# Attention feeding a balanced expert layer: a new order for the tiles, the q turns and the writes of the attention stage

## The chip, the cores and the metric

The kernel runs on one core of a Trainium2 chip. The metric is the device time of one execution in microseconds (us), and the median of several runs is compared. The profile is one more execution, taken by the hardware profiler; its times are in microseconds from the start of its span, except where ns is written. PE is TensorE (matmuls and transposes), DVE is VectorE, ACT is ScalarE, POOL is GpSimd, and SP is the engine whose queue issues most of the transfers.

## The reference

```python
# q, k, v: (8 batches, 8 heads, 576 rows, 64), float32
kv  = einsum('bhsd,bhse->bhde', k, v)            # a 64 x 64 matrix for each head, no softmax
out = einsum('bhsd,bhde->bhse', q, kv)
rms = sqrt(mean(out * out, axis=-1) + 1e-6)
x   = out / rms * g_norm                         # then (B, S, H*D) = 4608 tokens of 512
logits = x @ w_gate                              # 8 experts
# tokens go to experts greedily, best logit first, each expert takes exactly 576
for e in range(8):
    out[mask_e] = relu(x[mask_e] @ w1[e]) @ w2[e]  # 512 -> 1024 -> 512
```

## The kernel before

The kernel has three stages. The attention stage (the first 121 us of the profile) computes x, without the factor g_norm, and the logits. It writes x to the DRAM tensor `x_dram`. Then a search on VectorE finds the threshold of the first expert and its list of tokens. From about 160 us on, eight expert layers run on TensorE, each with rows gathered from `x_dram`; searches for the later experts run beside them. The change is in the attention stage.

There, `load` issues one transfer of 576 KB for half of the heads of q, k or v of one batch. Each of the six halves has two buffers. All loads and all writes of x go through SP's queue in program order, and `paced` lets each of them start only after the third one before it has landed. The loads of batches 0 and 1 are issued at the top. The later ones are issued by `again` inside `prepare`, two batches ahead, as soon as the buffer's last reader stands in the program.

`prepare(b)` is a generator that does all that batch b needs before its tiles:

- `sum_kv(r)`, for four pairs of heads, sums k-transposed times v into the PSUM tile `kv_ps` (L395). ScalarE copies the upper half of it as `odd` (L415), VectorE adds the lower half to make `kv` (L417), and GpSimd copies that into `kvx` (L423).
- `turn_q(n)`, for n from 0 to 4, transposes four blocks of q (two in the last) into the PSUM tile `qt_ps` (L380) and copies them into `qt`, on VectorE for n = 1 and 2 and on ScalarE else.
- `kv` is transposed into `t_ps` (L431), copied by ScalarE as `kvt` (L433), and multiplied by the gate's weights in `w_ps` (L442), which VectorE copies into the last 8 columns of `kvx` (L444). So one product of q with `kvx` gives the output and the parts of the logits.

`qt_ps`, `t_ps` and `w_ps` share the two PSUM buffers of the tag `tr`. The generator yields four times, and the main loop takes one piece of it after each tile.

`tiles(c0, rows)` gives the functions `one`, `scale` and `logits` for the tiles of a batch. A tile has 128 rows of a batch, all eight heads. A batch of 576 rows has four and a half, so every odd batch has a fifth tile, with the last 64 rows of the batch before it and its own. `one(t, ...)` makes 16 matmuls into `o_ps` (32 for the tile of two batches, L479); ScalarE squares them as `sq` (L485) and copies them into `o_sb` (L486); VectorE sums the squares into `ms` (L490). `scale` turns all sums of the batch into the factors `inv` (L494 to L498). `logits` adds up the logits `lg` (L503, L506), and multiplies `o_sb` by `inv` into `xo`: for batches 0 to 6 on GpSimd at once (L511), and for the last on ScalarE, put off until after the loop (`late`, L516). Writes of `xo` are collected in `writes` and issued when eight or more are waiting, the oldest first (L520).

`ones(n)` makes matmuls of constants whose result nobody reads (L361). `chore` runs one piece of a list of small VectorE work for the search: first its set-up, then, from batches 2, 4 and 6 on, `early` for nine columns of `lg` in four pieces; the last of these (L303, L335) compares them with 32 candidates into `over_c`. PE, DVE, ACT and SP take their instructions in the order of the program here; POOL's order is left to the scheduler.

The main loop is:

```python
for b in range(B):
    parts = prepare(b + 1) if b + 1 < B else iter(())
    ...
    for t in range(len(rows)):
        one(t, copies, {0: 1, 3: 2}.get(t, 0))
        next(parts, None)
        if b < 2 or t == 3 or b == 6 and t == 2:
            chore()
    ...
    scale()
    logits()
```

Of the kernel before, what the change touches and what calls it, by code (L numbers as in the profile page):

```python
# [7 lines left out]
FT = mybir.dt.float32  # L8
# [7 lines left out]
P = 128  # L16
# [10 lines left out]
def kernel(  # L27
# [14 lines left out]
    B, H, S, D = q.shape  # L42
# [4 lines left out]
    HP = P // 2  # L47
    R = S // HP
    GC = N // P
    DC = DM // P  # L50
    FC = F // P
    W = D + E
# [12 lines left out]
    att = att_cm.__enter__()  # L65
# [22 lines left out]
            loaded[name, b, h].rearrange("p r j d -> p r (j d)"),  # L88
            src[b].rearrange("h s d -> (h s) d").rearrange("(r p j) d -> p r (j d)", r=NP, j=R)[:, rs]))

    for b in range(2):
        for h in range(2):
            for name in "kvq":
                load(name, b, h)

    ones_b = asg.tile([P, P], BF, name="ones_b")
    nc.vector.memset(ones_b, 1.0)
# [252 lines left out]
    def chore(times=1):  # L350

        for _ in range(times):
            if chores:
                chores.pop(0)()
# [12 lines left out]
    def prepare(b):  # L367

        k_sb, v_sb, q_sb = ([loaded.pop((name, b, h)) for h in range(2)] for name in "kvq")
        q_sb = [x.rearrange("p r j d -> p (r j d)") for x in q_sb]  # L370
        NT = NP * R // 2
        qt = att.tile([P, 2, NT, HP], FT, name="qt", tag="qt", bufs=3)
        turned_q[b] = qt

        def turn_q(n):
            m = min(4, NT - 4 * n)
            t_ps = psa.tile([P, 4, P], FT, name="qt_ps", tag="tr", bufs=2)
            for x in range(m):
                h, at = divmod(4 * n + x, NT // 2)
                nc.tensor.transpose(t_ps[:, x, :], q_sb[h][:, at * P:(at + 1) * P], ident)  # L380

            to, got = qt[:, :, 4 * n:4 * n + m], t_ps[:, 0:m].rearrange("p x (l c) -> p l x c", l=2)
            if n in (1, 2):
                nc.vector.tensor_copy(to, got)
            else:
                nc.scalar.copy(to, got)


        kv_ps = psa.tile([P, 2, 512], FT, name="kv_ps", tag="kv")

        def sum_kv(r):
            for j in range(R):
                for l in range(2):
                    ls, cs = slice(l * D, (l + 1) * D), slice(j % 2 * D, (j % 2 + 1) * D)
                    nc.tensor.matmul(kv_ps[cs, l, r * D:(r + 1) * D], lhsT=k_sb[r // 2][ls, r % 2, j, :], rhs=v_sb[r // 2][ls, r % 2, j, :],  # L395
                                     start=(j < 2), stop=(j >= R - 2))

        def again(names, h):
            if b + 2 < B:
                for name in names:  # L400
                    load(name, b + 2, h)

        if b > 0:
            ones(2, kv_ps[:, 0, :])
        for r in range(2):
            sum_kv(r)
            if r:
                again("kv", 0)
            turn_q(r)
            yield  # L410
        sum_kv(2)
        sum_kv(3)
        again("kv", 1)
        odd = att.tile([D, 2, NP * D], FT, name="odd", tag="odd")
        nc.scalar.copy(odd, kv_ps[D:P, :, 0:NP * D])  # L415
        kv = att.tile([D, NP, 2, D], FT, name="kv", tag="kv")
        nc.vector.tensor_tensor(kv.rearrange("p r l d -> p l r d"),  # L417
                                kv_ps[0:D, :, 0:NP * D].rearrange("p l (r d) -> p l r d", d=D),
                                odd.rearrange("p l (r d) -> p l r d", d=D), op=AL.add)

        kvx = att.tile([P, H, W], FT, name="kvx", tag="kvx", bufs=3)
        for n in range(2):
            nc.gpsimd.tensor_copy(kvx[n * D:(n + 1) * D, :, 0:D], kv.rearrange("p r l d -> p (r l) d"))  # L423
        if b == 0:
            ones(5)
        yield
        turn_q(2)
        again("q", 0)
        t_ps = psa.tile([P, NP, D], FT, name="t_ps", tag="tr", bufs=2)
        for r in range(NP):  # L430
            nc.tensor.transpose(t_ps[:, r, :], kv[:, r].rearrange("p l d -> p (l d)"), ident[0:D, 0:D])  # L431
        kvt = att.tile([P, NP, D], FT, name="kvt", tag="kvt")
        nc.scalar.copy(kvt, t_ps)  # L433
        yield
        turn_q(3)
        if b == 0:
            nc.vector.tensor_scalar(gw.rearrange("p r l e -> p (r l e)"), in0=gw.rearrange("p r l e -> p (r l e)"),
                                    scalar1=g_col, scalar2=None, op0=AL.mult)
        w_ps = psa.tile([P, NP, 2 * E], FT, name="w_ps", tag="tr", bufs=2)
        for r in range(NP):  # L440
            for n in range(2):
                nc.tensor.matmul(w_ps[n * D:(n + 1) * D, r], lhsT=kvt[:, r, :],  # L442
                                 rhs=gw[:, r].rearrange("p l e -> p (l e)"), start=True, stop=True)
        nc.vector.tensor_copy(kvx[:, :, D:W], w_ps.rearrange("p r (l e) -> p (r l) e", l=2))  # L444
        kv_of[b] = kvx
        turn_q(4)
        again("q", 1)

    LAG = 4
    writes, late = [], []  # L450
    last_own = GC - (R + 1) // 2

    def tiles(c0, rows):


        T = len(rows)
        o_sb = att.tile([P, T, H, W], FT, name="o_sb", tag="o_sb", bufs=2)
        xo = att.tile([P, T, H, D], FT, name="xo", tag="xo", bufs=LAG + 1)
        ms = att.tile([P, T * H], FT, name="ms", tag="ms")
        rt = att.tile([P, T * H], FT, name="rt", tag="rt")  # L460
        inv = att.tile([P, T * H], FT, name="inv", tag="inv")
        own = c0 + T <= last_own

        def one(t, copies, fill):

            o_ps = psa.tile([P, 2, 512], FT, name="o_ps", tag="o", bufs=2)
            ones(fill, o_ps[:, 0, :])
            for r2 in range(NP // 2):
                for l in range(2):
                    for rp in range(2):  # L470
                        r = 2 * r2 + rp
                        at = [slice(h * HP, (h + 1) * HP) for h in range(2)]
                        halves = rows[t]
                        parts = [(slice(0, P), halves[0], 2)] if halves[0][0] == halves[1][0] else [
                            (at[n], half, 1) for n, half in enumerate(halves)]
                        for rows_at, (bn, j), m in parts:
                            block = R * r + j
                            ks = slice(block % 2 * D, (block % 2 + 1) * D)
                            nc.tensor.matmul(  # L479
                                o_ps[rows_at, rp, (2 * r2 + l) * W:(2 * r2 + l + 1) * W],  # L480
                                lhsT=turned_q[bn][ks, l, block // 2:block // 2 + m].rearrange("p x c -> p (x c)"),
                                rhs=kv_of[bn][ks, 2 * r + l], start=True, stop=True)
            o4 = o_ps[:, :, 0:NP * W].rearrange("p b (h w) -> p b h w", w=W)
            sq = att.tile([P, H, D], FT, name="sq", tag="sq")
            nc.scalar.activation(sq.rearrange("p (b h) d -> p b h d", b=2), o4[:, :, :, 0:D], ACT.Square, scale=D ** -0.5)  # L485
            copies.append(lambda: nc.scalar.copy(o_sb[:, t].rearrange("p (b h) w -> p b (h w)", b=2), o_ps[:, :, 0:NP * W]))  # L486
            if own or t != T - 2:
                while copies:
                    copies.pop(0)()
            nc.vector.reduce_sum(out=ms[:, t * H:(t + 1) * H], in_=sq, axis=AXX)  # L490
# [38 lines left out]
    with tc.manual_schedule(engines={PE, DVE, ACTE, SPE}):  # L529
        ones(18)  # L530
        for _ in prepare(0):
            pass
        for b in range(B):
            parts = prepare(b + 1) if b + 1 < B else iter(())
            rows = [((b, j), (b, j + 2)) for j in (0, 1, 4, 5)]
            if b % 2:
                rows.append(((b - 1, R - 1), (b, R - 1)))
            one, scale, logits = tiles(b // 2 * R + b % 2 * (R // 2), rows)
            copies = []
            if b in choose_at:  # L540
                early(*choose_at[b])
            for t in range(len(rows)):
                one(t, copies, {0: 1, 3: 2}.get(t, 0))
                next(parts, None)
                if b < 2 or t == 3 or b == 6 and t == 2:
                    chore()
            for _ in parts:
                pass
            if b + 1 == B:
                while chores:  # L550
                    chore()
            scale()
            logits()
            if b < B - 1:
                chore(2 if b == 6 else 1)

            while len(writes) >= 2 * LAG:
                writes.pop(0)()
        early(27, GC)
        while chores:  # L560
            chore()
        for do in late:
            do()
        while writes:
            writes.pop(0)()
# [683 lines left out]
```

## Time and profile before

| | |
|---|---|
| median of 3 runs | 658.64 us (658.54 to 659.15) |
| the profiled execution: its own time, its span | 660.36 us, 658.6 us |
| mean granted TensorE clock | 0.968 |
| busy: PE, DVE, ACT, POOL | 605.8, 387.8, 194.5, 389.3 us |
| read from HBM, written | 71.32 MB, 18.87 MB |
| loads of q, k, v: 48 transfers | 576 KB each, 5.8 to 6.1 us from issue to landing |
| writes of x: 20 transfers | 512 or 256 KB, 4.0 to 4.4 us |

A line of the timeline has the start, the duration, the engine, the line of the program, the operation, what is written and from what, the shape, the count, and in brackets how long the engine had been idle before it and what ended that. In the windows table each stretch has the busy time of each engine in it, then the clock that was granted to TensorE as a share of full speed, the share of time that the DMA engines were busy, and the rate. The search stage and the attention stage have different limits, so shares of the whole span say little about either.

### The profile page before, as it was taken

The page shows a single profiled execution, that of the slowest core. Times are in us where ns is not written, and L with a number is a line of the kernel's source. Part 1 is how long each engine was busy: PE and PEld are TensorE (multiplying, and loading weights), DVE is VectorE, ACT ScalarE, POOL GpSimd, SP SyncE. Part 2 cuts the span into 40 slices and gives each one's busy share as a digit, 9 for nine tenths or more (in the row PEclk, how much of TensorE's full clock was granted, in tenths as well). Part 3 has the DMA queues.
Part 4 walks back from the last instruction along what each step waited for, and adds up shares of the span by engine and source line. Part 5 has one row for each costly group of instructions (what it writes and reads, how often), then busy time and mean ns, then how long its engine had stood idle before and what let it go on. Part 6 is the DMA issues. An engine that isn't in the chain of part 4 may idle for free.

```text
span 658.6 us, 12759 instructions
## 1 busy us (share of the span) xinstructions
PE 605.8 (92%) x4932; PEld 464.6 (71%) x4932; DVE 387.8 (59%) x1249; ACT 194.5 (30%) x395; POOL 389.3 (59%) x405
## 2 busy tenths in 40 slices
PE   7989998335899999999999999999999999999994
PEld 4767777232678677867786786778678867877873
DVE  4466667778678588668757956976671053123201
ACT  1555665611131223123212222231223123222300
POOL 1035434104585487749846974887388669848822
PEclk9999999657999999999999999999999999999998
DMA  8999989416306402710442072109103620721001
GB/s 270 310 315 295 292 291 340 154 50 199 128 0 204 164 33 71 257 41 33 158 171 73 1 262 99 41 0 323 46 32 100 229 72 1 279 84 37 0 9 64
DMA packets 49852, 91.02 MB, mean 138 GB/s; under 512 B 3712, under 2 KB 20096, under 8 KB 49792
## 3 DMA queue, kind: packets, MB, share of 16 engines
q1 hardware_dynamic: 43200, 71.31, 31.6%
q0 software_dynamic: 5888, 18.88, 8.3%
q8 instruction: 39, 0.64, 0.4%
q14 instruction: 21, 0.17, 0.1%
q10 hardware_dynamic: 704, 0.02, 0.1%
HBM read 71.32 MB, written 18.87 MB: 137 GB/s over the span
## 4 chain that ended last, share of the span: by engine, by line
PE 77%; DVE 9%; DMA 5%; issue 4%; ACT 3%; POOL 1%; POOLq 0%; SPq 0%; DVEq 0%; ACTq 0%
PE x_ps L1065 13%; PE x_ps L1025 11%; PE z_ps L1065 9%; PE y_ps L1065 9%; PE z_ps L1025 7%; PE y_ps L1025 7%; PE o_ps L479 4%; PE y_ps L1127 4%; PE kv_ps L395 3%; PE t_ps L969 3%; PE qt_ps L380 2%; DMA v_sb<-in_v_dram 2%; DMA q_sb<-in_q_dram 2%; PE given_ps L651 1%; PE given_ps L646 1%
## 5 line engine op out<-in xcount | busy, mean ns | idle before, releaser
L1070 ACT COPY h<-x_ps 128x288 f32<-128x288 f32 x93 | 37.2, 400 | 166.5 <-PE x_ps L1065 153.7
L1065 PE MATMUL x_ps<-xs,sw 128*128 128x288 f32 x248 | 71.3, 409 | 0.0
L875 POOL DMA_INDIRECT xg<-x_dram,ids x40 | 38.1, 952 | 51.8 <-DMA w_sb<-in_moe_w_dram 37.7
L992 POOL DMA_INDIRECT out_dram<-y_sb,outs x32 | 31.5, 983 | 55.8 <-DVE y_sb L1163 41.1
L1025 PE MATMUL x_ps<-tw,sh 128*128 128x256 f32 x256 | 61.6, 384 | 0.0
L972 ACT ACTIVATE xt<-t_ps,g_col 128x512 f32<-128x512 f32 (+1 forms) x40 | 25.7, 645 | 110.9 <-PE t_ps L969 110.9
L1065 PEld LDWEIGHTS x_ps<-xs,sw 128*128 128x128 f32 x248 | 46.2, 190 | 14.3 <-issue 1.7
L955 POOL TENSOR_TENSOR sw<-w_sb 128x256 f32<-128x256 f32 x64 | 46.8, 731 | 12.3 <-PE z_ps L1065 9.6
L1017 POOL TENSOR_TENSOR sh<-hid 128x512 f32<-128x512 f32 x32 | 40.7, 1272 | 19.9 <-ACT hid L1040 19.9
L1025 PEld LDWEIGHTS x_ps<-tw,sh 128*128 128x128 f32 x256 | 46.9, 190 | 7.1 <-issue 0.8
L1040 ACT ACTIVATE hid<-hid 128x576 f32<-128x576 f32 x64 | 43.8, 686 | 22.9 <-DVE hid L1079 13.1
L511 POOL TENSOR_TENSOR xo<-o_sb,inv 128x512 f32<-128x512 f32 x31 | 32.9, 1090 | 29.7 <-DVE inv L498 16.6
L1103 POOL TENSOR_TENSOR tw<-w_sb 128x512 f32<-128x512 f32 x32 | 40.1, 1276 | 5.0 <-DMA w_sb<-in_moe_w_dram 5.0
L479 PEld LDWEIGHTS o_ps<-kvx,qt 64*128 64x128 f32 (+1 forms) x640 | 33.7, 181 | 12.0 <-issue 7.1
L479 PE MATMUL o_ps<-kvx,qt 64*128 64x72 f32 (+1 forms) x640 | 38.9, 274 | 3.4 <-ACT o_sb L486 3.4
L1065 PE MATMUL z_ps<-xt,sw 128*128 128x288 f32 x128 | 37.8, 413 | 0.1
L1065 PE MATMUL z_ps<-xs,sw 128*128 128x288 f32 x128 | 37.0, 409 | 0.0
L1065 PE MATMUL x_ps<-xt,w_sb 128*128 128x288 f32 x124 | 36.8, 414 | 0.1
L1065 PE MATMUL y_ps<-xt,w_sb 128*128 128x288 f32 x128 | 36.9, 409 | 0.0
L1065 PE MATMUL y_ps<-xs,w_sb 128*128 128x288 f32 x128 | 36.7, 408 | 0.0
L490 DVE TENSOR_REDUCE ms<-sq 128x8 f32<-128x512 f32 x36 | 24.3, 683 | 20.1 <-ACT sq L485 19.8
L423 POOL COPY kvx<-kv 64x512 f32<-64x512 f32 x16 | 9.7, 607 | 43.9 <-DVE kv L417 26.9
(278 smaller groups left out, 1332.4 us busy)
## 6 DMA issues: line engine op xcount, KB each, us to landing
w_sb<-in_moe_w_dram SPq DMA_DIRECT2D x32, 512.0 KB, 5.7
w_sb<-in_moe_w_dram SPq DMA_DIRECT2D x8, 2048.0 KB, 14.3
k_sb<-in_k_dram SPq DMA_DIRECT2D x16, 576.0 KB, 5.8
v_sb<-in_v_dram SPq DMA_DIRECT2D x16, 576.0 KB, 5.8
q_sb<-in_q_dram SPq DMA_DIRECT2D x16, 576.0 KB, 6.1
x_dram<-xo SPq DMA_DIRECT2D x16, 512.0 KB, 4.4
x_dram<-xo SPq DMA_DIRECT2D x4, 256.0 KB, 4.0
xg<-x_dram,ids POOLq DMA_INDIRECT x40, 5.4
```

What stands on the lines that cost most here:

```text
L479: nc.tensor.matmul(o_ps[rows_at, rp, (2 * r2 + l) * W:(2 * r2 + l + 1) * W], lhsT=turned_q[bn][ks, l, block // 2:block // 2 + m].rearrange ...
L511: nc.gpsimd.tensor_tensor(xo[:, t], o_sb[:, t, :, 0:D], inv[:, t * H:(t + 1) * H].rearrange("p (h o) -> p h o", o=1).to_broadcast([P, H, D ...
L875: tokens = nc.gpsimd.indirect_dma_start(out=xg[0:nr], out_offset=None, in_=x_dram, in_offset=bass.IndirectOffsetOnAxis(ap=ids[0:nr, n:n + ...
L955: in_order(nc.gpsimd.tensor_tensor(o, x, y, op=op))
L992: put = nc.gpsimd.indirect_dma_start(out=out, out_offset=bass.IndirectOffsetOnAxis(ap=ids_of[t][0:nr, n:n + 1], axis=0), in_=y_sb[0:nr, :] ...
L1017: in_order(nc.gpsimd.tensor_tensor(o[:, ms], x[:, ms], y[:, ms], op=op))
L1025: nc.tensor.matmul(p_ps[:, n], lhsT=left[:, f, n * P:(n + 1) * P], rhs=right[:, f], start=first, stop=(f == FH - 1), skip_group_check=True)
L1040: nc.scalar.activation(both, both, ACT.Relu)
L1065: nc.tensor.matmul(p_ps, lhsT=lhs[:, r], rhs=rhs[:, r], start=(m in (1, 2, 4, 5) and r == 0), stop=(r == 1), skip_group_check=(m in (6, 7, ...
L1070: nc.scalar.copy(u, p_ps)
L1103: in_order(nc.gpsimd.tensor_tensor(o, x, y, op=AL.subtract))
L1127: nc.tensor.matmul(y_ps[l * nr:(l + 1) * nr], lhsT=hid[:, l * FH + f, a:a + nr], rhs=w2[:, l * FH + f, :], start=(f == 0), stop=(f == FH - 1))
```

## The change

- **Loads**: of batch 1, the halves of q are loaded after those of k and v.
- **Turning q**: for all batches but the first, `turn_q(0)` comes after the fourth kv sum, 1 and 2 together after `kvt`, 3 before `w_ps` and 4 at the end. For batch 0 there is one turn in each piece. `prepare` has one yield fewer.
- **Order of tiles**: an odd batch begins with the tile of two batches. `qt` and `kvx` have two buffers instead of three.
- **x**: `xo` has six buffers instead of five. x of batches 6 and 7 is multiplied by ScalarE after the loop. Writes are issued only at the end of rounds 4 and 5, and after the loop; the loads all stand ahead of them.
- **ones**: in `one`, a single one ahead of the first and the fourth tile in batches 0 to 2 and none in later ones, in place of one and two in every batch. The two in `prepare` stay.
- **Chores**: batch 6 has one after each tile; there is none at the end of it.

```diff
--- before.py
+++ after.py
@@ -88,10 +88,9 @@
             loaded[name, b, h].rearrange("p r j d -> p r (j d)"),
             src[b].rearrange("h s d -> (h s) d").rearrange("(r p j) d -> p r (j d)", r=NP, j=R)[:, rs]))
 
-    for b in range(2):
-        for h in range(2):
-            for name in "kvq":
-                load(name, b, h)
+    for b, order in enumerate(("kvqkvq", "kvkvqq")):
+        for n, name in enumerate(order):
+            load(name, b, int(name in order[:n]))
 
     ones_b = asg.tile([P, P], BF, name="ones_b")
     nc.vector.memset(ones_b, 1.0)
@@ -369,7 +368,7 @@
         k_sb, v_sb, q_sb = ([loaded.pop((name, b, h)) for h in range(2)] for name in "kvq")
         q_sb = [x.rearrange("p r j d -> p (r j d)") for x in q_sb]
         NT = NP * R // 2
-        qt = att.tile([P, 2, NT, HP], FT, name="qt", tag="qt", bufs=3)
+        qt = att.tile([P, 2, NT, HP], FT, name="qt", tag="qt", bufs=2)
         turned_q[b] = qt
 
         def turn_q(n):
@@ -400,14 +399,21 @@
                 for name in names:
                     load(name, b + 2, h)
 
+        turns = [[0], [1], [2], [3], [4]] if b == 0 else [[], [0], [1, 2], [3], [4]]
+
+        def turn_some():
+            for n in turns.pop(0):
+                turn_q(n)
+                if n in (2, 4):
+                    again("q", n // 2 - 1)
+
         if b > 0:
             ones(2, kv_ps[:, 0, :])
-        for r in range(2):
-            sum_kv(r)
-            if r:
-                again("kv", 0)
-            turn_q(r)
-            yield
+        sum_kv(0)
+        sum_kv(1)
+        again("kv", 0)
+        turn_some()
+        yield
         sum_kv(2)
         sum_kv(3)
         again("kv", 1)
@@ -418,21 +424,21 @@
                                 kv_ps[0:D, :, 0:NP * D].rearrange("p l (r d) -> p l r d", d=D),
                                 odd.rearrange("p l (r d) -> p l r d", d=D), op=AL.add)
 
-        kvx = att.tile([P, H, W], FT, name="kvx", tag="kvx", bufs=3)
+        kvx = att.tile([P, H, W], FT, name="kvx", tag="kvx", bufs=2)
         for n in range(2):
             nc.gpsimd.tensor_copy(kvx[n * D:(n + 1) * D, :, 0:D], kv.rearrange("p r l d -> p (r l) d"))
+        turn_some()
         if b == 0:
             ones(5)
         yield
-        turn_q(2)
-        again("q", 0)
         t_ps = psa.tile([P, NP, D], FT, name="t_ps", tag="tr", bufs=2)
         for r in range(NP):
             nc.tensor.transpose(t_ps[:, r, :], kv[:, r].rearrange("p l d -> p (l d)"), ident[0:D, 0:D])
         kvt = att.tile([P, NP, D], FT, name="kvt", tag="kvt")
         nc.scalar.copy(kvt, t_ps)
+        turn_some()
         yield
-        turn_q(3)
+        turn_some()
         if b == 0:
             nc.vector.tensor_scalar(gw.rearrange("p r l e -> p (r l e)"), in0=gw.rearrange("p r l e -> p (r l e)"),
                                     scalar1=g_col, scalar2=None, op0=AL.mult)
@@ -443,25 +449,24 @@
                                  rhs=gw[:, r].rearrange("p l e -> p (l e)"), start=True, stop=True)
         nc.vector.tensor_copy(kvx[:, :, D:W], w_ps.rearrange("p r (l e) -> p (r l) e", l=2))
         kv_of[b] = kvx
-        turn_q(4)
-        again("q", 1)
-
-    LAG = 4
+        turn_some()
+
+    HELD = 6
     writes, late = [], []
-    last_own = GC - (R + 1) // 2
+    last_own = GC - R
 
     def tiles(c0, rows):
 
 
         T = len(rows)
         o_sb = att.tile([P, T, H, W], FT, name="o_sb", tag="o_sb", bufs=2)
-        xo = att.tile([P, T, H, D], FT, name="xo", tag="xo", bufs=LAG + 1)
+        xo = att.tile([P, T, H, D], FT, name="xo", tag="xo", bufs=HELD)
         ms = att.tile([P, T * H], FT, name="ms", tag="ms")
         rt = att.tile([P, T * H], FT, name="rt", tag="rt")
         inv = att.tile([P, T * H], FT, name="inv", tag="inv")
         own = c0 + T <= last_own
 
-        def one(t, copies, fill):
+        def one(t, copies, fill, wait):
 
             o_ps = psa.tile([P, 2, 512], FT, name="o_ps", tag="o", bufs=2)
             ones(fill, o_ps[:, 0, :])
@@ -484,7 +489,7 @@
             sq = att.tile([P, H, D], FT, name="sq", tag="sq")
             nc.scalar.activation(sq.rearrange("p (b h) d -> p b h d", b=2), o4[:, :, :, 0:D], ACT.Square, scale=D ** -0.5)
             copies.append(lambda: nc.scalar.copy(o_sb[:, t].rearrange("p (b h) w -> p b (h w)", b=2), o_ps[:, :, 0:NP * W]))
-            if own or t != T - 2:
+            if not wait:
                 while copies:
                     copies.pop(0)()
             nc.vector.reduce_sum(out=ms[:, t * H:(t + 1) * H], in_=sq, axis=AXX)
@@ -539,10 +544,11 @@
             copies = []
             if b in choose_at:
                 early(*choose_at[b])
-            for t in range(len(rows)):
-                one(t, copies, {0: 1, 3: 2}.get(t, 0))
+            order = range(len(rows)) if b % 2 == 0 else [len(rows) - 1] + list(range(len(rows) - 1))
+            for n, t in enumerate(order):
+                one(t, copies, 1 if b < 3 and n in (0, 3) else 0, b + 1 == B and n == len(rows) - 2)
                 next(parts, None)
-                if b < 2 or t == 3 or b == 6 and t == 2:
+                if b < 2 or n == 3 or b == 6:
                     chore()
             for _ in parts:
                 pass
@@ -551,10 +557,10 @@
                     chore()
             scale()
             logits()
-            if b < B - 1:
-                chore(2 if b == 6 else 1)
-
-            while len(writes) >= 2 * LAG:
+            if b < B - 2:
+                chore()
+
+            while b in (B - 4, B - 3) and writes:
                 writes.pop(0)()
         early(27, GC)
         while chores:
```

## The prediction, before the change was run

> **What bounds the kernel now.** I call "round b" the work of one pass of the loop over `b`: tiles of batch b, interleaved with `prepare(b + 1)`. The profile's own execution took 660.36 us with a span of 658.6; the median of the runs is 658.64, so 1.72 of what I sum lies outside a typical run and I subtract gains from the median. The page's first lists put TensorE at 92% and 77% of the chain that ended last, but that averages two stages. So next I read the windows table: until 110 us DMA is busy 0.9 to 0.96 and PE 0.8 to 1.0 of each stretch; between 120 and 150 DMA is 0.01 to 0.28 and PE 0.25 to 0.5 (the search for the expert). Two resources look full in the attention stage; which one ends last, PE's timeline with its idle notes says:
>
> ```profile
> 36.08 0.63 PE L380 MATMUL qt_ps<-ident,q_sb 128*128 128x128 f32 x4 [1.65 <-DMA q_sb<-in_q_dram]
> ...
> 101.60 0.66 PE L380 MATMUL qt_ps<-ident,q_sb 128*128 128x128 f32 x4 [0.94 <-DMA q_sb<-in_q_dram]
> ...
> 120.05 1.24 PE L479 MATMUL o_ps<-kvx,qt 64*64 64x72 f32 x32 [2.98 <-ACT o_sb L486]
> ```
>
> After round 0 begins at 18.45, PE waits only 2.6 us for DMA in the whole stage, always for q; DMA is full but nearly hidden. The largest wait is the third line, in the last round. VectorE's timeline shows what was late there:
>
> ```profile
> 114.94 1.11 DVE L303 TENSOR_TENSOR best<-pick,code_mx 128x72 bf16<-128x72 f32 x1
> 115.96 2.22 DVE L335 TENSOR_TENSOR over_c<-mx,cand 128x192 bf16<-128x192 f32 x2
> 118.10 2.08 DVE L490 TENSOR_REDUCE ms<-sq 128x8 f32<-128x512 f32 x3
> ```
>
> Three `ms` reductions stand behind a chore, so ScalarE's `sq` buffers, then its PSUM copies, then PE's next tile are late. GpSimd multiplies xo from 113.81 to 118.06. The same comparison is short later, when GpSimd is idle (127.44, 0.45 us for 288 columns). Last, SP's queue:
>
> ```profile
> 81.90 4.52 SPq L520 DMA_DIRECT2D x_dram<-xo  x3
> 88.69 0.37 SPq L87 DMA_DIRECT2D k_sb<-in_k_dram  x1
> ...
> 99.35 35.15 SPq L520 DMA_DIRECT2D x_dram<-xo  x17
> ```
>
> Only 3 of 20 writes stand ahead of loads: the loads of batch 7 start at 88.69, 6.8 us after the first write.
>
> **The skill.** *SBUF — State Buffer*, section "SBUF: two separate sides", says VectorE with two SBUF inputs and GpSimd take one shared port pair in turn, whole instructions at a time. The trace agrees: the comparisons take about 1.1 us each (2.22 for two), a GpSimd multiply 1.09. *TensorE: Matmul & The Clock Gate*, "Why this matters for your kernels", says an idle gap of about 3 us drops TensorE to half clock. Here the clock fell 1.5 us into the 2.98 us gap (1.00 until 118.5, 0.50 from 118.75), yet not in the 1.65 us gap at 34.4. Its Part 4 says transposes do not count as busy in the same way; no trace here separates that.
>
> **Bricks**, from starts on PE's timeline: full tile 1.05 us, two-batch tile 0.66, 36 kv matmuls 0.73, 72 of them 1.31, `turn_q` 0.59 (the last 0.28), t_ps 0.40, w_ps 0.60, one `ones` matmul 0.27. Rounds 0 to 6 start at 18.45, 31.73, 46.49, 59.17, 72.23, 84.92, 97.97, and round 7 at 111.66; its last tile ends at 121.29. Lengths: 13.28, 14.76, 12.68, 13.06, 12.69, 13.05, 13.69, 9.63. An even round holds 11.15 of bricks with the two `ones` of `prepare`, 0.81 of three more, and 0.7 of waits; an odd one 0.66 more tile and 0.41 of waits.
>
> **Part by part.**
>
> *Ones.* 3 per round become 2 in rounds 0 to 2 (-0.27 each) and 0 later (-0.81 each).
>
> *New order inside a round.* Turn 0 moves behind the fourth kv sum, turns 1 and 2 behind t_ps. All `qt_ps`, `t_ps`, `w_ps` share two PSUM slots, so turn 2 waits for `kvt`, which ScalarE copies after `sq` (0.6) and `o_sb` (0.6): 0.52 us (now: 0.53, even rounds only, covered by the two-batch tile in odd ones). Turn 4 waits for a copy out of the slot: 0.34 (now 0.1 and 0.41). The two-batch tile at the head of an odd round needs turn 4 only from its 20th matmul: about 0.1, bound 0 to 0.45 if its first matmul waits. Without other delays: even rounds 11.15+0.86 = 12.0, odd 11.81+0.96 = 12.8; rounds 0 to 2 carry 0.54 of `ones` more. The preparation of batch 0 gains nothing: it waits for v until 12.77, and turn 1 now comes after that (+0.2).
>
> *q loaded later.* In batch 1 q goes behind k and v; used one stage later, it is 1.7 us early in round 1 (lands 35.9, turned near 37.6): the 1.65 wait goes. Next late is nothing on DMA: from batch 4 on, k lands over 5 us ahead.
>
> *Writes behind the loads.* SP passes the last load before any write; batch 7's loads gain about 6 us, so the 0.94 us wait goes. 12 writes leave at the end of round 4, 3 at that of round 5; SP lags by design, and all are behind loads, so nothing queued needs them. Six xo buffers: batch 6 reuses batch 0's, written by about 100 us, long before its multiplies.
>
> *x of batch 6 on ScalarE.* 32 more multiplies by 0.241 (40 took 124.49 to 134.14) = 7.7 us. Cover: ScalarE is idle until 161.64. SP's last write moves from 134.2 to about 142 less the stage's gain, still before the index at 149.9 less the same gain, with SP's weight loads queued behind. Gathers came at 155.78. Cost 0; were the cover gone, up to 7.7.
>
> *A wait added.* An even round now begins right after a full tile, so `scale()` ends about 0.95 later, while kv is wanted 2.8 us sooner (turns 0 and 1 no longer stand before the sums). VectorE runs reductions, logits and a chore first. After an odd round the chore is a comparison: 1.3 us in round 4 (kv about 0.95 late, of which 0.52 replaces the kvt wait: +0.43) and 2.22 us in round 6, plus that round's new first chore of 0.6: kv 2.4 late. Behind kv stand t_ps, three turns, w_ps; with later queueing I take +2.6 (bounds 0.5, if the multiplies start later and don't block, and 4, if the clock also falls).
>
> *Round 7.* Chores of 18 to 27 now finish in round 6 and GpSimd has no xo of batch 6, so the stall goes. Then ScalarE sets the pace: start to last tile's end 5.85 by its `sq` and copies (now 9.63): -3.8. The tail after it, 6.65 to given_ps at 127.94, stays.
>
> **Sum**: +0.2, rounds 0 to 6: -0.3, -1.55, -0.1, -0.3, -0.25, -0.3, +0.9, round 7: -3.8; together -5.5. One cold stretch of PE of 3.4 us costs about 1.2 (the cold two-batch tile took 1.24, 0.73 warm); at one chance in two, +0.6. So -4.9: **653.7 us** of 658.64 (655.5 of the profiled 660.36). What follows the search moves as it is.
>
> **Rivals.** *The stall only moves* (657 to 660): round 6 loses 4 us to kv and the two-batch tile waits 0.45 in each odd round, so about 4 of the 5 us come back. For it: over_c's 2.22; against: round 7's 2.98 wait has no successor. 658.
>
> *More is won* (under 650.5): chores in round 6 miss the multiplies, costing 0.5 instead of 2.6, and no cold stretch: 653.7-2.1-0.6-0.3 = 650.7 or less.
>
> *The clock, slower*: the removed `ones` held TensorE at full clock in rounds 3 to 7. A window of 3.4 us at half clock costs about 1.6 us if full of matmuls; three or four eat the gain, and half the windows of 51 us (7 or 8) give 653.7+12 = 666. Against it: 48.38 to 54.41 has no `ones` and shows 1.00. For it: after the change 11 us pass without.
>
> *It does little of what it says*: q and the writes are hidden, but for 2.6 us; then 656.
>
> **Chances.** The forecast and its neighbours from 650.5 to 657, 0.54; more won, 0.12; the stall moves, 0.16; slower by the clock or by a wait that I don't see, 0.18. A measurement tells 0.2% (1.3 us) from no change: faster 0.73, same 0.09, slower 0.18. Range 649.5 to 661: outside are a far win (0.07) and the worse half of the slower cases (0.13).
>
> **What would show it.** Right: no wait for q after 18 us; PE's gap in round 7 under 1 us; over_c in round 6, short; 72 multiplies on ScalarE; all loads issued before any write; rounds 3 and 5 about 12.8 long; t_ps in round 6 waiting about 2.5 us for kv. Wrong: clock below 1.00 before round 6, a gather that waits for x_dram, or a weight load held by SP's writes.

## The result, and the profile after

| | before | after |
|---|---|---|
| median in the comparison (21 runs each) | 660.09 us | 664.23 us |
| range of the runs | 657.67 to 665.42 | 660.41 to 674.85 |
| ratio of undisturbed runs, 95% interval | | 1.0049 [1.0028, 1.0070] |
| the profiled execution: its own time, its span | 660.36, 658.6 us | 662.49, 660.6 us |
| mean granted TensorE clock | 0.968 | 0.953 |

The change makes the kernel slower, by about 3 us (0.49% of 660), where 4.9 us less was forecast. The ratio leaves out runs whose clock was disturbed further, so it is not the ratio of the medians. Within the 18 runs after that it counts, the time follows the run's mean clock (correlation -0.87): 660.4 us goes with 0.963, 669.9 us with 0.942.

First PE's timeline of the kernel after: start, duration, line, operation, and the idle time before it with what ended that.

```profile
9.81 0.63 PE L379 MATMUL qt_ps<-ident,q_sb 128*128 128x128 f32 x4 [0.43 <-DMA q_sb<-in_q_dram]
12.81 2.40 PE L394 MATMUL kv_ps<-v_sb,k_sb 64*64 64x64 f32 x72 [2.38 <-DMA v_sb<-in_v_dram]
15.14 1.11 PE L379 MATMUL qt_ps<-ident,q_sb 128*128 128x128 f32 x4
...
39.79 1.04 PE L394 MATMUL kv_ps<-v_sb,k_sb 64*64 64x64 f32 x52 [0.68 <-issue]
...
108.75 0.46 PE L436 MATMUL t_ps<-ident,kv 64*128 64x64 f32 x4 [2.37 <-DVE kv L423]
109.14 1.19 PE L379 MATMUL qt_ps<-ident,q_sb 128*128 128x128 f32 x8
110.26 1.39 PE L484 MATMUL o_ps<-kvx,qt 64*128 64x72 f32 x16
111.58 1.11 PE L379 MATMUL qt_ps<-ident,q_sb 128*128 128x128 f32 x4
...
114.61 8.30 PE L484 MATMUL o_ps<-kvx,qt 64*64 64x72 f32 x96
```

Read the durations as well as the waits. The second line waits 2.38 us for v, and then its 72 matmuls take 2.40 where they took 1.38 before. The four transposes behind it take 1.11, not 0.66. The same happens from 111 us on, a little after a wait of 2.37 us for kv: round 7, the last line, takes 8.30 us. No line in the stage waits for q after 18 us.

The windows table of the kernel after shows why. The last three columns are the granted clock, the DMA share and the rate.

```profile
11.00:13.00 2.00, 0.19 (x8) 0.19 (x12) 0.00 (x0) 0.06 (x1) 0.00 (x0) 0.74 1.01 354
13.00:16.00 3.00, 3.00 (x76) 2.87 (x74) 0.13 (x1) 0.58 (x1) 0.00 (x0) 0.50 0.91 280
16.00:19.00 3.00, 2.72 (x11) 1.08 (x9) 1.15 (x2) 0.00 (x0) 1.21 (x2) 0.54 0.93 334
...
60.00:80.00 20.00, 18.29 (x480) 15.61 (x480) 13.62 (x30) 12.53 (x26) 7.78 (x9) 1.00 0.93 309
...
106.00:110.00 4.00, 1.63 (x19) 1.30 (x18) 3.93 (x10) 1.50 (x3) 3.33 (x5) 1.00 0.76 287
110.00:114.00 4.00, 3.67 (x40) 2.94 (x38) 2.40 (x8) 1.63 (x3) 0.03 (x1) 0.62 0.87 328
114.00:118.00 4.00, 4.00 (x54) 3.53 (x56) 2.93 (x10) 1.82 (x5) 0.00 (x0) 0.50 0.00 0
```

In stretches of 0.05 us the clock is 0.50 from 11.96 to 18.79 us and from 110.95 to 158.73; before, only from 118.62 to 156.17, when 2.7 us were left to the end of PE's last tile. PE full at 0.50, as in 114 to 118, is the loss itself.

What came late before the second gap, the one for kv, is on VectorE's timeline of the kernel after:

```profile
104.02 2.22 DVE L334 TENSOR_TENSOR over_c<-mx,cand 128x96 bf16<-128x96 f32 x2
...
108.02 0.67 DVE L423 TENSOR_TENSOR kv<-kv_ps,odd 64x512 f32<-64x512 f32 x1
...
114.00 0.52 DVE L334 TENSOR_TENSOR over_c<-mx,cand 128x192 bf16<-128x192 f32 x2
```

GpSimd multiplies xo from 102.75 to 108.14, across the first pair of comparisons (2.22 us); the later pair, twice as wide, takes 0.52 with GpSimd idle. kv stands behind the first pair in VectorE's queue. SP's queue and ScalarE after the loop:

```profile
90.63 51.74 SPq L525 DMA_DIRECT2D x_dram<-xo  x20
152.75 2.13 SPq L834 DMA_DIRECT2D w_sb<-in_moe_w_dram  x4
```

```profile
124.74 17.27 ACT L521 ACTIVATE xo<-o_sb,inv 128x64 f32<-128x64 f32 x72
```

All 20 writes stand behind the loads; the last is issued at 142.4, 10 us ahead of what SP issues next, and the first gather goes out at 157.82. That cover held.

### The profile page after: what moved, and what is told of

Its sections match the earlier page's. It is cut to its first block, busy times and chain, and to the rows that moved or that the text cites. A ratio compares the mean times of both kernels' runs of the same rounds, so it can differ in the third digit from the quotient of the medians.

```text
span 660.6 us, 12738 instructions
## 1 busy us (share of the span) xinstructions
PE 605.1 (92%) x4902; PEld 469.1 (71%) x4914; DVE 385.9 (58%) x1249; ACT 201.9 (31%) x427; POOL 384.9 (58%) x401
## 4 chain that ended last, share of the span: by engine, by line
PE 76%; DVE 11%; issue 4%; DMA 3%; ACT 3%; POOL 1%; POOLq 0%; SPq 0%; DVEq 0%; ACTq 0%
PE x_ps L1071 13%; PE x_ps L1031 11%; PE z_ps L1071 9%; PE y_ps L1071 9%; PE y_ps L1031 7%; PE z_ps L1031 7%; PE o_ps L484 5%; PE y_ps L1133 4%; PE t_ps L975 3%; PE qt_ps L379 2%; PE kv_ps L394 2%; DMA v_sb<-in_v_dram 2%; PE given_ps L657 1%; DVE ms L495 1%; ACT sq L490 1%
## 5 line engine op out<-in xcount | busy, mean ns | idle before, releaser
L516 POOL TENSOR_TENSOR xo<-o_sb,inv 128x512 f32<-128x512 f32 x27 | 28.7, 1091 | 40.4 <-DVE inv L503 40.4
L484 PE MATMUL o_ps<-kvx,qt 64*128 64x72 f32 (+1 forms) x640 | 42.1, 290 | 0.4
L484 PEld LDWEIGHTS o_ps<-kvx,qt 64*128 64x128 f32 (+1 forms) x640 | 37.4, 195 | 5.6 <-issue 4.8
L1163 ACT COPY u<-x_ps 128x512 f32<-128x512 f32 x24 | 14.0, 582 | 67.2 <-PE x_ps L1031 60.2
```

What stands on the lines that cost most here:

```text
L484: nc.tensor.matmul(o_ps[rows_at, rp, (2 * r2 + l) * W:(2 * r2 + l + 1) * W], lhsT=turned_q[bn][ks, l, block // 2:block // 2 + m].rearrange ...
L516: nc.gpsimd.tensor_tensor(xo[:, t], o_sb[:, t, :, 0:D], inv[:, t * H:(t + 1) * H].rearrange("p (h o) -> p h o", o=1).to_broadcast([P, H, D ...
```

## The experiments

After the result I held this theory, **A**: two waits that the change makes, at the start and in round 6, each drop the clock, and what follows runs at half speed. The rival, **B**: the missing `ones` let the clock fall, as the prediction's own slower case said. A `ones(9)` is nine constant matmuls, 2.11 us at full clock. Ratios are to the kernel before, from five rounds.

**e1: fill the gap at the start.**

```diff
 turn_some()
+if b == 0: ones(9)
 yield
```

> Batch 0 alone gets nine more ones matmuls behind its first turn, in the gap in which TensorE waits for the second v half (10.4 to 12.8 us in the changed kernel). Theory A (the clock falls because of two waits, this one and the one for kv in round 6, and each fall makes cold what follows): the clock stays 1.00 through 8 to 20 us, the first tile of round 0 starts near 18.9 instead of 21.8, and the whole gets about 2.8 us shorter (ratio to before from 1.005 to about 1.0005); round 6 and its clock as in the changed kernel. Rival B (the clock fell for want of ones in the later rounds): the start may be mended, no more than 3 us. Rival C (the two start losses are the longer waits themselves, not the clock): round 0 starts where it did, 21.5 to 21.8, and nothing is gained.

Measured: 1.0019 [0.9992, 1.0047]. PE's timeline of e1:

```profile
10.13 2.11 PE L360 MATMUL ones_ps<-wide,ones_b 128*128 128x512 bf16 x8
12.73 1.38 PE L394 MATMUL kv_ps<-v_sb,k_sb 64*64 64x64 f32 x72 [0.50 <-DMA v_sb<-in_v_dram]
...
26.21 1.76 PE L394 MATMUL kv_ps<-v_sb,k_sb 64*64 64x64 f32 x49 [2.07 <-issue]
```

The sums are at full clock again (1.38), and round 0 begins at 18.73 instead of 21.47. The ratio falls by 2 us (1.0049 to 1.0019), but the two intervals overlap. In this profile round 0 runs into a pause of 2.07 us in the middle of a kv sum, and the clock is at 0.50 from 26.07 to 29.48. In round 6 it still falls, at 111.40.

**e2: take the comparison away from GpSimd's multiplies.** In an odd round the chore at the end becomes one after the fifth tile, ahead of `scale`.

```diff
-if b < 2 or n == 3 or b == 6:
+if b < 2 or n >= 3 or b == 6:
...
-if b < B - 2:
+if b < B - 2 and (b < 2 or b % 2 == 0):
```

> The fourth chore of the columns of batches 2 to 5 (the comparison into over_c) is taken after the fifth tile of the odd round, ahead of scale, instead of after logits, where GpSimd multiplies xo. Theory A: the comparison takes about 0.5 us instead of 2.2, t_ps in round 6 waits under 0.8 us for kv instead of 2.37, the clock stays 1.00 until the last tile, round 6 is near 12.5 us (15.0) and round 7 near 6 (8.3): about 5 us less, ratio about 0.997. Rival B (want of ones): the clock still falls in one of the rounds 3 to 7. Rival C (kv is late for the order of the round, whatever the chore does): the wait stays over 1.5 us.

Measured: 0.9949 [0.9921, 0.9976]. VectorE's and PE's timelines of e2:

```profile
99.54 0.52 DVE L334 TENSOR_TENSOR over_c<-mx,cand 128x96 bf16<-128x96 f32 x2
```

```profile
105.11 0.46 PE L436 MATMUL t_ps<-ident,kv 64*128 64x64 f32 x4 [0.26 <-DVE kv L423]
...
109.97 2.04 PE L484 MATMUL o_ps<-kvx,qt 64*64 64x72 f32 x48
112.24 2.17 PE L484 MATMUL o_ps<-kvx,qt 64*128 64x72 f32 x32 [0.23 <-ACT o_sb L491]
114.78 1.11 PE L484 MATMUL o_ps<-kvx,qt 64*128 64x72 f32 x16 [0.37 <-ACT o_sb L491]
```

The comparison of rounds 3 and 5, taken ahead of the multiplies, brings 1% (1.0049 to 0.9949, 6.6 us). In round 6 the wait for kv is 0.26 and the clock stays at 1.00 until 117, so that round 7 takes 5.92 us (109.97 to 115.89); in round 4 a wait for kv of 0.78 is gone. The start is as in the change, but in this profile the clock did not fall there:

```profile
12.73 1.38 PE L394 MATMUL kv_ps<-v_sb,k_sb 64*64 64x64 f32 x72 [2.47 <-DMA v_sb<-in_v_dram]
```

**e3: all `ones` back.**

```diff
-1 if b < 3 and n in (0, 3) else 0
+{0: 1, 3: 2}.get(n, 0)
```

> The changed kernel with the ones of before again: one ahead of the first tile and two ahead of the fourth in every round. Theory A: 18 matmuls of 0.27 us come back, 4.9 us of TensorE's time, some of it inside waits; the clock still falls at the start and in round 6, where the wait for kv is under 0.3 us shorter; the time is the same or up to 4 us longer. Rival B (the missing ones let the clock fall): the clock stays up from round 3 to the end and the time falls by about 3 us or more.

Measured: 1.0020 [0.9985, 1.0055], an interval that overlaps the change's own. PE's timeline of e3:

```profile
108.84 0.46 PE L436 MATMUL t_ps<-ident,kv 64*128 64x64 f32 x4 [1.90 <-DVE kv L423]
...
111.30 1.99 PE L484 MATMUL o_ps<-kvx,qt 64*128 64x72 f32 x16
```

With all `ones` in place the clock falls in round 6 all the same, at 110; the next tile takes 1.99 instead of 1.11. B falls as an account of round 6. The gap at the start was 2.38 us, and here too the clock stayed up.

**e4: e1 and e2 together.**

> The first and the second edit together. Theory A: the clock is 1.00 from start to the last tile, gains add up: about 7.5 us under the changed kernel, ratio to before about 0.993, and the spread of the runs shrinks to that of before. Rival B: the clock still falls in rounds 3 to 7 in some runs and the spread stays.

Measured: 0.9920 [0.9893, 0.9946], 8.5 us under the changed kernel; the clock is at 1.00 from the start to 115.5, inside the last tile. Both gaps gone, this kernel beats the one before by about 5 us, the size that was forecast. How much of that is the new order, e5 asks.

**e10: the wait stays, the clock is kept.** This separates the two costs of round 6: kv is as late as in the change, but PE computes constants meanwhile.

```diff
+if b == 7: ones(9)
 t_ps = psa.tile(...)
```

> The changed kernel with nine ones matmuls ahead of t_ps in round 6, where TensorE waits 2.37 us for kv. The wait stays as long, only filled. Theory A (part of the loss is the clock that falls in this wait): t_ps starts at the same distance from the round's start (about 9.2 us), the clock stays 1.00 until the last tile, round 6 is near 14.3 instead of 15.0, round 7 near 6.1 instead of 8.3, and about 3 us come back: ratio near 1.000. Rival (lateness of kv alone, whatever the clock): nothing changes.

Measured: 0.9980 [0.9952, 1.0009]. PE's timeline of e10:

```profile
106.12 2.12 PE L360 MATMUL ones_ps<-wide,ones_b 128*128 128x512 bf16 x9
108.65 0.43 PE L438 MATMUL t_ps<-ident,kv 64*128 64x64 f32 x4 [0.41 <-DVE pick L297]
...
113.17 2.04 PE L486 MATMUL o_ps<-kvx,qt 64*64 64x72 f32 x48
115.44 2.17 PE L486 MATMUL o_ps<-kvx,qt 64*128 64x72 f32 x32 [0.23 <-ACT o_sb L493]
117.98 1.11 PE L486 MATMUL o_ps<-kvx,qt 64*128 64x72 f32 x16 [0.37 <-ACT o_sb L493]
```

The comparison is still 2.22 us and `t_ps` starts as late after the start of its round as in the change (9.36 us against 9.27), but the clock holds until 120: round 6 takes 13.9 us instead of 15.13, round 7 5.9 instead of 8.30. That is 3.6 us in the profile and 4.6 (0.69%) by the ratios. In its profile the clock did fall in the start's gap of 2.32 us.

**e5: the old kernel with the new place of chores alone.**

```diff
-if b < 2 or t == 3 or b == 6 and t == 2:
+if b < 2 or t == 3 or b == 6:
...
-if b < B - 1: chore(2 if b == 6 else 1)
+if b < B - 2: chore()
```

> The kernel before, with one chore after each tile of round 6 and none at its end. Theory A (round 7's stall came from the comparison of columns 18 to 26 meeting GpSimd's multiplies): the comparison is done in round 6 at about 0.5 us, TensorE's wait of 2.98 us in round 7 goes, and the whole is 3 to 4 us shorter, ratio about 0.995. Rival (ScalarE's copies set round 7's pace and the stall only moves): within 1 us of before.

Measured: 0.9934 [0.9908, 0.9959]. VectorE's and PE's timelines of e5:

```profile
106.58 2.22 DVE L335 TENSOR_TENSOR over_c<-mx,cand 128x96 bf16<-128x96 f32 x2
...
114.73 0.52 DVE L335 TENSOR_TENSOR over_c<-mx,cand 128x192 bf16<-128x192 f32 x2
```

```profile
116.13 2.01 PE L479 MATMUL o_ps<-kvx,qt 64*128 64x72 f32 x32
118.53 1.11 PE L479 MATMUL o_ps<-kvx,qt 64*128 64x72 f32 x16 [0.39 <-ACT o_sb L486]
...
120.11 1.78 PE L479 MATMUL o_ps<-kvx,qt 64*128 64x72 f32 x48
```

The last line has no wait any more where 2.98 us stood. This one edit, worth 0.66% or 4.4 us, is what the prediction counted for round 7 (3.8). It also means that e4 (0.9920) is not clearly better than the old order with this edit alone (0.9934). In the old order the slow comparison of round 6 delays nobody, because kv is not wanted then.

**e6: e4 without the two `ones` of `prepare` from batch 4 on.**

```diff
-if b > 0:
+if 0 < b <= 3:
     ones(2, kv_ps[:, 0, :])
```

> The kernel with both edits, and no ones at all from round 3 on: the two ahead of the kv sums go in rounds 3 to 6. Theory A (only waits of about 2 us or more make the clock fall): the clock stays 1.00 from round 3 to the last tile, and 8 matmuls of 0.27 us go: 2.2 us less than with both edits, ratio about 0.989. Rival B (the ones hold the clock): it falls between 60 and 110 us and the time grows by 3 us or more.

Measured: 0.9893 [0.9867, 0.9919], the best of all; in its profile the clock is at 1.00 until 116.7, behind the last tile. With no `ones` from round 3 to the end, the new order can keep its clock.

**e7: the old kernel with the new `ones` alone.**

```diff
-{0: 1, 3: 2}.get(t, 0)
+1 if b < 3 and t in (0, 3) else 0
```

> The kernel before with this one part of the change: one ones matmul ahead of the first and the fourth tile in batches 0 to 2, none in later ones. Theory A: 18 matmuls of 0.27 us go, 3 to 4.9 us less, since the waits for q and in round 7 take some back; clock as before, 1.00 until round 7. Rival B: the clock falls between rounds 3 and 6, and the time is the same or longer.

Measured: 0.9997 [0.9966, 1.0029], so the expected gain did not come. PE's timeline of e7:

```profile
80.60 0.46 PE L431 MATMUL t_ps<-ident,kv 64*128 64x64 f32 x4
81.52 1.05 PE L380 MATMUL qt_ps<-ident,q_sb 128*128 128x128 f32 x4 [0.46 <-ACT kvt L433]
...
84.09 1.99 PE L479 MATMUL o_ps<-kvx,qt 64*128 64x72 f32 x16
```

A's forecast was wrong here, and B right for the old order: the clock falls at 81.64 after a wait of only 0.46 us, and is back at 88.46. Its fastest run, 655.84, against 657.67 or more before, suggests that the gain is there in a run where the clock holds. Between the tile that ends at 79.66 and `w_ps` at 82.50 the old order has transposes alone, 2.8 us of them with their wait; in the new order a tile stands between the turns. The Trainium skill (*TensorE: Matmul & The Clock Gate*, "Part 4: PE-mode transpose") says that transposes do not count as busy in the same way. That fits, but one profile doesn't settle it.

**e8 and e9: what the two changes to x are worth**, each undone in e4: x of batch 6 back on GpSimd (e8), writes issued as soon as eight are waiting (e9).

```diff
-last_own = GC - R
+last_own = GC - (R + 1) // 2
```

> The kernel with both edits, but x of batch 6 is multiplied by GpSimd at once, as before the change, and only that of batch 7 on ScalarE. Theory A (once no chore with two inputs is left in round 7, GpSimd's multiplies there block nothing): within 1.5 us of the kernel with both edits; ScalarE's late multiplies are 40 again and SP's last write comes 7 to 8 us earlier, with nothing gained. Rival (moving x of batch 6 is what frees round 7): round 7 goes from 6.2 to over 8 us.

```diff
-while b in (B - 4, B - 3) and writes:
+while len(writes) >= 8:
```

> The kernel with both edits, but writes of x are issued as in the kernel before, the oldest when eight or more are waiting, so that some stand ahead of the last loads. Theory A (DMA has several us of slack by then): within 1 us of the kernel with both edits. Rival (holding the writes is what the later rounds live on): k or q of batch 7 late in round 6, 1 to 4 us more.

Measured: e8 0.9946 [0.9920, 0.9972], e9 0.9931 [0.9904, 0.9959], against e4's 0.9920 [0.9893, 0.9946]. Neither differs from e4 by what could be measured. SP's queue of e9 has writes ahead of loads again:

```profile
81.32 5.53 SPq L527 DMA_DIRECT2D x_dram<-xo  x3
87.79 0.37 SPq L87 DMA_DIRECT2D k_sb<-in_k_dram  x1
```

Yet between 24 and 98 us no line of PE in e9 waits for a load: with q wanted later, the loads no longer need to pass the writes.

**e12: turn 2 later, in e6**, so that it no longer waits for `kvt`.

```diff
-[[], [0], [1, 2], [3], [4]]
+[[], [0], [1], [2, 3], [4]]
```

> The kernel without ones from round 3 on, with turn 2 moved behind the next tile, next to turn 3, in batches 1 to 7. Theory A (the wait of 0.4 to 0.75 us before turn 2 is for the PSUM slot that kvt empties): it goes in six or seven rounds, 2.5 to 4 us less, ratio near 0.984. Rival D (four turns and w_ps in a row, with no tile between, count for little as work and let the clock fall, as in the kernel before with few ones): the clock falls somewhere from 50 to 105 us and the runs spread upwards; the same or longer.

Measured: 0.9928 [0.9897, 0.9958], nothing gained on e6. PE's timeline of e12 shows the successor:

```profile
77.43 1.09 PE L379 MATMUL qt_ps<-ident,q_sb 128*128 128x128 f32 x8
79.22 0.65 PE L450 MATMUL w_ps<-gw,kvt 128*64 128x16 f32 x16 [0.69 <-ACT qt L385]
```

The wait of 0.56 us for `kvt` is gone, and `w_ps` waits 0.69 for its slot, behind ScalarE's copy of turn 3. That is not all. The profiled run (652.38 us, mean clock 0.968, at 1.00 until 113) is one of the fastest of 22; the median run has a mean clock of 0.957, where that of e6 has 0.966. So in many runs the clock fell more than in the profile, as rival D expects; where, no profile shows.

## Why the prediction was wrong, point by point

The forecast for the profiled execution was 655.5; it took 662.49, so 7.0 us are to be accounted for. Where they are, in the prediction's own terms:

| term | predicted | measured | missed by |
|---|---|---|---|
| round 0 begins | 18.65 | 21.47 | +2.8 |
| round 1 | 13.2 | 14.22 | +1.0 |
| rounds 0 and 2 to 5 | | | +0.3 |
| round 6 | 14.6 | 15.13 | +0.5 |
| round 7 | 5.85 | 8.30 | +2.45 |
| cold stretch of round 6, priced apart | 0.6 | in rounds 6 and 7 | -0.6 |
| after round 7 | 0 | +0.5 | +0.5 |

- **The step that failed most is the price of the clock**, "one cold stretch of PE of 3.4 us costs about 1.2 (...); at one chance in two, +0.6". By its own two tile times the sum gives 1.4 (3.4 x (1 - 0.73/1.24)), and under the rivals it says 1.6, but that is the small part. The wait before it was sized well: 2.37 us for kv where 2.4 was written, behind an `over_c` of 2.22 as written. The clock fell in all three profiles whose kv was late in round 6 with the wait unfilled (after, e1, e3), and it did not come back in round 7, though PE was busy all through it (4.00 us of 114 to 118). PE's matmuls at half clock, not ScalarE's copies, then set round 7's pace: ScalarE waits 0.5 to 1.1 us for each tile. The prediction had priced 3.4 us of half clock, and it was the 12 us from 110.95 to the last tile. e10 measures the term: 3.6 us in the profile, 4.6 by the ratio, for the 0.6 that was set.
- **The start, "+0.2", left out the clock.** The prediction saw that turn 1 moves behind v. It didn't ask what had filled PE before v came: a sum and a turn, 1.3 us, in the middle of that idle time. With both sums joined ahead, PE idles 2.38 us in one piece; in the profile the clock fell 1.5 us into it, and sums, turns and `ones` ran at half clock until 18.79. The order itself costs what was written: in e2 and e3, where the same gap did not drop the clock, round 0 begins at 18.72 and 18.85, for 18.65. The clock fell in two of the four profiles with the gap (after, e10) and in none of the six where `ones` fill it (e1, e4, e6, e8, e9, e12). Where it falls it costs 2.7 us (after) or 1.5 (e10).
- **Round 1, "-1.55", brought -0.54.** The wait for q went, as predicted. But PE pauses in the middle of a sum: 0.68 us at 39.79. The profile names no releaser ("issue"); by its timing, told in the last section, it is a late fetch of instructions, which the prediction did not have at all. Beside it stands the kvt wait, 0.62.
- **Round 7's stall** went by moving the chores, as the sum said: e5 alone shows it. In the change itself the gain is hidden by the clock; in e2 and e10 round 7 takes 5.9 us, the predicted 5.85.
- **The bricks, the odd rounds and the tail** held: rounds 3 and 5 took 12.9 for 12.8, round 4 12.2 for 12.4; `given_ps` comes 6.65 us after the last tile, as before. ScalarE's longer multiplies and SP's later writes cost nothing, for the reason given. But the writes behind the loads and x of batch 6 on ScalarE also brought nothing that e8 and e9 could measure.
- **The rival that came nearest was the clock, for the wrong reason.** It blamed the removed `ones`; e3 and e6 show that in the new order they are not what keeps the clock, and e2 and e10 that in round 6 the unfilled wait is what drops it. Only in the old order (e7) do they seem to hold the clock. Of the three signs named for "wrong", the first came true, a clock below 1.00 before round 6, though at the start and not in rounds 3 to 5, where it had been looked for. The signs named for "right" came true as well, the 2.37 us for kv among them: they ask for waits, places and the odd rounds, and none asks how long rounds 6 and 7 take.

Joined, with the gap filled, the comparison moved and the spare `ones` gone (e6), the new order is 1.07% faster than the old [0.81, 1.33]. The chores' place alone gives 0.66% of that in the old order (e5). What the order, the loads and the fewer `ones` add is 0.41%, about 2.7 us, and the intervals of e5 and e6 still overlap.

## What to carry to other kernels

When a move leaves TensorE idle for about 2 us in one piece, price what follows at half clock as well as the wait itself: here 3.4 us (e1, e10), 6.8 (the start, e7), 10.2 (e5), 13.7 (e8), and all 12 us that were left of rounds 6 and 7. When work is moved off a wait, ask what other waits it had been filling. Keep two-input VectorE work whose result the next stage waits for clear of GpSimd's bursts: here the place of the comparisons in two rounds was worth 1%.

## What the runs showed of the hardware

- The same gap does not always drop the clock, and the profiles show why. In each of the thirteen, all changes of the clock lie on one grid with a step of 3.41 us, and the grid's position differs from profile to profile. After the change the clock falls at 11.96, is back at 18.79, falls at 110.95 and is back at 158.73: 2, 27 and 14 steps. What counts is how PE's work falls into the steps. After the change PE is busy for 1.46 us of the step from 8.55 to 11.96, and the clock falls at its end. In e2 the gap is as long, but two steps share it, with PE busy for 2.01 and 1.89 us, and the clock stays. In round 1 of the kernel before a wait of 1.65 us leaves 1.76 us busy in its step and the clock stays; in e5 a wait of 1.75 leaves 1.51, and it falls. The Trainium skill (*TensorE: Matmul & The Clock Gate*, Part 1, "What's actually happening") describes such a free-running window of about 3.4 us, and names about 3.4 us of sustained work for the return; the traces agree with the first, and round 7's 8.3 us at half clock with PE full show that the second is not enough. The section "Why this matters for your kernels" advises against gaps over about 3 us; here waits of 1.75 (e5) to 2.38 us (the start) dropped the clock, and the measurement decides.
- The kind of work seems to count, though no run varied it alone. In the attention stage the clock came back seven times, each time after a step with 1.7 to 2.9 us of kv sums or `ones`. Twenty steps in which PE was busy for 2.8 us or more at half clock, but with tiles, turns and `w_ps` and at most 0.75 us of sums or `ones`, did not bring it back; neither did one with 2.40 us of sums in which PE stood idle for 0.85. Behind the late kv of round 6 the change has only tiles, turns and `w_ps`. Why these count for less, no run shows.
- Half clock does not double everything: 72 kv matmuls 2.40 against 1.38, a tile 1.99 against 1.11, four transposes 1.11 against 0.66.
- Pauses of PE without a releaser ("issue") follow fetches of instructions. The page lists a queue q8 of the kind "instruction", with transfers of 16 KB. All 22 such pauses of 0.35 us or more between 18 and 125 us, in eleven profiles, end 1.2 to 1.6 us after one of these has landed: in e1 it lands at 24.68 and PE goes on at 26.21, after the change at 38.56 and 39.79. Every profile of the new order has one or two of them in the kv sums, the old order (before, e5, e7) has none there. That the late fetch is the cause is read from this timing; no run changed it.
